# Windowed attention and a gated convolution feed-forward on one core: pairs of 64-token tiles and engine queues from a table

## The chip, the cores and the metric

One core of a Trainium2 chip runs the whole program in one launch. The metric is the device time of a run in microseconds; of several runs the median is taken. The engines have short names here: PE is TensorE (matrix products into PSUM), DVE is VectorE, ACT is ScalarE, POOL is GpSimd, SP is SyncE, whose queue issues nearly all DMAs.

## The reference

The inputs are q, k, v of shape (8, 8, 576, 64) (batch, head, token, feature) and three weights. All are fp32, and so is the output, (8, 576, 512).

```python
# attention within 32 tokens on either side
scores = q @ k.T / sqrt(64)
scores = where(abs(pos_q - pos_k) <= 32, scores, -1e9)
attn = exp(scores - max); attn = attn / (sum(attn) + 1e-9)
x = concat_heads(attn @ v)                      # (8, 576, 512)
# gated feed-forward with a convolution of three taps over the tokens
h = relu(x @ w_in)                              # w_in (512, 1024)
c = conv_w[0]*h[t-1] + conv_w[1]*h[t] + conv_w[2]*h[t+1]   # zero beyond a batch's ends
y = (h * sigmoid(c)) @ w_out                    # w_out (1024, 512)
```

## The kernel before

**Attention** goes by pairs of heads (`g`, 32 in all: 8 batches of 4 pairs). The 576 tokens are nine tiles of 64 queries, and each needs the 128 keys from 32 before its first token on. `load_qk` (L103) brings q or k of four heads in one DMA, with nine neighbouring tokens in one run; `load_v` (L95) brings v in blocks of 128 tokens, shifted by 32. `cast` (L109) turns each loaded tile into bf16 on POOL. Odd tiles need v shifted by 64 more tokens: `shift_v` copies `ve` to `vo` by two DMAs a batch (on DVE for batch 0). `job_tr` (L229, L236) transposes q or k of four heads by matmuls with an identity, nine for each pair of heads; ACT and DVE each copy one half out of PSUM. `job_sc` (L257 to L268) does 18 score matmuls for a pair of heads into one tile of three PSUM banks (`pa`) and one bank (`pf`), ACT takes the exponential (1088 and 64 columns), DVE multiplies by the mask. `job_av` (L282 to L301) does 20 matmuls; a column of ones in v gives the sum; DVE takes the reciprocal and scales into `xn`. `job_xt` (L312 to L324) transposes x to `xT`, by PE for batches 0 and 1 and by a DMA transpose for the others.

**Feed-forward** goes by chunks of 384 tokens (12) and blocks of 128 hidden features (`m`, 8 to a chunk). `job_ph` (L349 to L369) is four matmuls and a relu on ACT into `hT`. `job_pc` (L387 to L392) does the three taps of the convolution as three matmuls with diagonal weights, ACT takes tanh into an fp32 tile `tn` in SBUF, and DVE makes the gate product `(tn + 1) * hT`, with the halves of the sigmoid folded into the weights. `job_py` (L405 to L412) is eight matmuls for each 128 tokens, a copy on ACT and a store.

**Order.** Each job has a due time written by hand and a list of jobs that come before it; `give_out` hands the jobs out in the order of these times. In the first stage the order of instructions on PE, ACT and DVE is fixed (`InOrder`, whose calls all show as L87), later the scheduler of the framework may move them. POOL and SP keep the order in which the jobs are handed out. PSUM tiles come from two pools: one of three banks and five of one bank.

Of the kernel before, what the change touches and what calls it, by code (L numbers as in the profile page):

```python
# [9 lines left out]
FP32 = mybir.dt.float32  # L11
BF16 = mybir.dt.bfloat16
AF = mybir.ActivationFunctionType
ALU = mybir.AluOpType


@with_exitstack
def kernel(
# [21 lines left out]
    CH = 2 * S // 3  # L40
    HW = CH // 2
    PAD = 32
    RP = S // 64

    consts = ctx.enter_context(tc.tile_pool(name="consts", bufs=1))
    pp = ctx.enter_context(tc.tile_pool(name="pp", bufs=1))
    apool = ctx.enter_context(tc.tile_pool(name="apool", bufs=3))
    fpool = ctx.enter_context(tc.tile_pool(name="fpool", bufs=2))
    spool = ctx.enter_context(tc.tile_pool(name="spool", bufs=3))
    psum_a = ctx.enter_context(tc.tile_pool(name="psum_a", bufs=1, space=bass.MemoryType.PSUM))  # L50
    psum_f = ctx.enter_context(tc.tile_pool(name="psum_f", bufs=5, space=bass.MemoryType.PSUM))

    NLD = 2
    NPH = NP // 2
    qkst = [[pp.tile([128, 2, RP, 64], FP32, name=f"{n}st{i}") for i in range(NPH)] for n in "qk"]
    vst = pp.tile([128, NBLK, H, 64], FP32, name="vst")
    qkb_pp = [
        [[pp.tile([128, RP, 2, 64], BF16, name=f"{n}b{i}{j}") for j in range(NPH)] for n in "qk"]
        for i in range(NLD)
    ]  # L60
    ve_pp = [pp.tile([128, NBLK, H, 65], BF16, name=f"ve{i}") for i in range(NLD)]
    vo_pp = [pp.tile([128, NBLK - 1, H, 65], BF16, name=f"vo{i}") for i in range(NLD)]
    NKT = 4
    kT_pp = [pp.tile([128, S + 2 * PAD], BF16, name=f"kT{i}") for i in range(NKT)]
    hT_pp = [pp.tile([128, MB, CH + (4 if i == 1 else 2)], BF16, name=f"hT{i}") for i in range(3)]

    w_in_sb = consts.tile([128, KC, d_ff], BF16, name="w_in_sb")
    w_out_sb = consts.tile([128, MB, d_model], BF16, name="w_out_sb")
    conv_w_sb = consts.tile([128, 3, MB], FP32, name="conv_w_sb")
    diag_w = consts.tile([128, 3, MB, 128], BF16, name="diag_w")  # L70
    ident = consts.tile([128, 128], BF16, name="ident")
    mask = consts.tile([128, 2 * S], BF16, name="mask")
    mask1 = consts.tile([128, NT, 64], BF16, name="mask1")

    fixed = tc.keep_in_program_order

    class InOrder:


        on = False  # L80

# [3 lines left out]
        def __getattr__(self, name):  # L85
            do = getattr(self.engine, name)
            return (lambda *args, **kwargs: fixed(do(*args, **kwargs))) if InOrder.on else do  # L87

    vector, scalar, tensor = InOrder(nc.vector), InOrder(nc.scalar), InOrder(nc.tensor)

    def load_v(b, c):

        lo = 128 * c - PAD
        s0, s1 = max(0, lo), min(S, lo + 128)
        fixed(nc.sync.dma_start(  # L95
            vst[s0 - lo:s1 - lo, c, :, :], v[b, :, s0:s1, :].rearrange("h p d -> p h d")
        ))

    def load_qk(b, y, i):


        src = (q, k)[y][b, 4 * i:4 * i + 4, :, :]
        fixed(nc.sync.dma_start(  # L103
            qkst[y][i].rearrange("p e j d -> p e (j d)"),
            bass.AP(src.tensor, src.offset, [[RP * D, 128], [2 * S * D, 2], [1, RP * D]]),
        ))

    def cast(out_, in_):
        fixed(nc.gpsimd.tensor_scalar(  # L109
            out=out_, in0=in_, scalar1=1.0, scalar2=0.0, op0=ALU.mult, op1=ALU.add  # L110
        ))

    def load_stream(b):

        i = b % NLD
        ve, vo = ve_pp[i], vo_pp[i]

        def cast_v(c):
            cast(ve[:, c, :, 0:64], vst[:, c, :, :])
            if b == 0 and c > 0:  # L120
                vector.tensor_copy(vo[0:64, c - 1, :, :], ve[64:128, c - 1, :, :])
                vector.tensor_copy(vo[64:128, c - 1, :, :], ve[0:64, c, :, :])

        of_qk = [
            (lambda y=y, j=j: load_qk(b, y, j),
             lambda y=y, j=j: cast(qkb_pp[i][y][j].rearrange("p j e d -> p e j d"), qkst[y][j]))
            for j in range(NPH) for y in range(2)
        ]
        of_v = [(lambda c=c: load_v(b, c), lambda c=c: cast_v(c)) for c in range(NBLK)]
        return of_qk + of_v  # L130

    def shift_v(b):

        ve, vo = ve_pp[b % NLD], vo_pp[b % NLD]
        for p0, src in ((0, ve[64:128, 0:NBLK - 1]), (64, ve[0:64, 1:NBLK])):
            fixed(nc.sync.dma_start(vo[p0:p0 + 64], src))


    nc.vector.memset(vst[0:PAD, 0, :, :], 0.0)
    nc.vector.memset(vst[128 - PAD:128, NBLK - 1, :, :], 0.0)  # L140
    loads0 = list(load_stream(0))
    for ld, _ in loads0:
        ld()
    conv_w24 = consts.tile([3 * MB, 128], FP32, name="conv_w24")
    nc.scalar.dma_start(conv_w24, moe_conv_w.rearrange("k (m p) -> (k m) p", p=128))
    make_identity(nc, ident)
    ident24 = consts.tile([3 * MB, 3 * MB], FP32, name="ident24")
    nc.vector.tensor_copy(out=ident24, in_=ident[0:3 * MB, 0:3 * MB])
    nc.vector.memset(mask1, 1.0)
    nc.gpsimd.affine_select(  # L150
        out=mask1, in_=mask1, compare_op=ALU.is_ge, fill=0.0, base=0,
        pattern=[[0, NT], [-1, 64]], channel_multiplier=1,
    )
    nc.gpsimd.affine_select(
        out=mask1, in_=mask1, compare_op=ALU.is_ge, fill=0.0, base=64,
        pattern=[[0, NT], [1, 64]], channel_multiplier=-1,
    )
    nc.vector.memset(mask1[0:PAD, 0, :], 0.0)
    nc.vector.memset(mask1[128 - PAD:128, NT - 1, :], 0.0)
    for e in range(2):  # L160
        nc.vector.tensor_copy(
            out=mask[:, 512 * e:512 * e + 512], in_=mask1[:, 0:8, :].rearrange("p t x -> p (t x)")
        )
        nc.vector.tensor_copy(out=mask[:, 1024 + 64 * e:1088 + 64 * e], in_=mask1[:, 8, :])
    for t_ in ve_pp + vo_pp[0:1]:
        nc.vector.memset(t_[:, :, :, 64], 1.0)
    for t_ in kT_pp:
        nc.vector.memset(t_[:, 0:PAD], 0.0)
        nc.vector.memset(t_[:, PAD + S:], 0.0)
    nc.vector.memset(hT_pp[0][:, :, 0], 0.0)  # L170
    nc.vector.memset(hT_pp[1][:, :, HW + 1:HW + 3], 0.0)
    nc.vector.memset(hT_pp[2][:, :, CH + 1], 0.0)
    def make_diag(m):
        for kk in range(3):
            vector.tensor_scalar(
                out=diag_w[:, kk, m, :], in0=ident,
                scalar1=conv_w_sb[:, kk, m:m + 1], scalar2=None, op0=ALU.mult,
            )

    def load_weight(src, dst, rows, cast_):  # L180

        n = src.shape[1] // 2
        for x in (0, n):
            st = {}

            def load(x=x, st=st):
                t_ = fpool.tile([128, rows * n], FP32, name="wst", tag="wst")
                st[0] = t_.rearrange("p (c f) -> p c f", c=rows)
                fixed(nc.sync.dma_start(
                    st[0], src.rearrange("(c p) f -> p c f", p=128)[:, :, x:x + n]  # L190
                ))

            def casts(x=x, st=st):
                step = 512 // n
                for c in range(0, rows, step):
                    cast_(dst[:, c:c + step, x:x + n], st[0][:, c:c + step])

            yield load, casts


    def slot_a():
        return psum_a.tile([128, 1536], FP32, name="pa", tag="pa")

    def slot_f():
        return psum_f.tile([128, 512], FP32, name="pf", tag="pf")

    xT, xn = {}, {}
    state = {}

    def job_tr(g2, y):  # L210

        b, i = g2 // NPH, g2 % NPH
        nat = qkb_pp[b % NLD][y][i]
        to = []
        for g in (2 * g2, 2 * g2 + 1):
            if y == 0:
                t_ = apool.tile([128, S], BF16, name="qT", tag="qT", bufs=4)
                to.append(t_)
            else:
                t_ = kT_pp[g % NKT]  # L220
                to.append(t_[:, PAD:PAD + S])
            state["qk"[y], g] = t_

        small = b == 0
        for js in ((range(0, 4), range(4, 8), range(8, RP)) if small else (range(RP),)):
            j0, n = js[0], len(js)
            ps = slot_f() if small else slot_a()
            for j in js:
                tensor.matmul(  # L229
                    ps[:, 128 * (j - j0):128 * (j - j0) + 128],  # L230
# [352 lines left out]
```

## Time and profile before

| | |
|---|---|
| runs (us) | 270.17, 272.04, 279.48; median 272.04 |
| profiled execution: span | 271.7 |
| instructions | 6447 |
| granted clock of PE over the span | 0.978 |
| HBM read, written | 32.52 MB, 9.44 MB |
| issues on SP | q and k 32, v 40, `vo` shifts 14, DMA transposes 30, weights 4, stores 36 |

The profiled execution has a span of 271.7 us, 0.3 us below the median of the runs. A busy time counts each moment once, although neighbouring instructions of an engine overlap a little. Weight loads of PE (PEld) overlap its matmuls. Idle time of an engine that doesn't bound a stage costs nothing there.

### The profile page before, as it was taken

How to read it: one execution, taken by the hardware profiler on the slowest of the kernel's cores; microseconds unless marked ns; L12 is line 12 of the kernel's file. 1: busy time of each engine (PE TensorE's matmuls, PEld its weight loads, DVE VectorE, ACT ScalarE, POOL GpSimd, SP SyncE). 2: the span in 40 equal slices, each digit the busy share in tenths (PEclk: the TensorE clock that was granted, in tenths of full speed). 3: DMA queues.
4: the chain of work that ended last, by engine and by line, in shares of the span. 5: the costliest groups of instructions: out<-in, count | busy, mean ns of one | idle time of the engine just before them, and what ended most of it. 6: DMA issues, size and time to landing. Idle time of an engine off the chain costs nothing.

```text
span 271.7 us, 6447 instructions
## 1 busy us (share of the span) xinstructions
PE 236.4 (87%) x2535; PEld 143.5 (53%) x2562; DVE 160.5 (59%) x362; ACT 175.3 (65%) x370; POOL 81.0 (30%) x96
## 2 busy tenths in 40 slices
PE   1736974786999978998999999999999999999994
PEld 1625543574665544554555556565656455555551
DVE  5797385895466673765766656676666562323230
ACT  2755572585577663876777777777778567657552
POOL 5758656873026201233323432322300000000000
PEclk9999998998999997999999999999999999999998
DMA  7999999997377986399959988967546114312123
GB/s 258 256 344 358 198 296 321 224 309 164 100 183 253 222 151 165 110 287 242 208 146 319 159 196 257 294 112 177 152 121 89 40 41 109 98 39 77 41 77 116
DMA packets 70498, 49.64 MB, mean 183 GB/s; under 512 B 53676, under 2 KB 55748, under 8 KB 70468
## 3 DMA queue, kind: packets, MB, share of 16 engines
q1 hardware_dynamic: 70432, 49.22, 70.6%
q8 instruction: 20, 0.33, 0.6%
q14 instruction: 10, 0.08, 0.1%
q10 hardware_dynamic: 36, 0.01, 0.0%
HBM read 32.52 MB, written 9.44 MB: 154 GB/s over the span
## 4 chain that ended last, share of the span: by engine, by line
PE 68%; DMA 15%; DVE 5%; SPq 4%; ACT 3%; issue 2%; POOL 0%
PE pf L405 22%; PE pf L349 20%; PE pf L387 14%; DMA kst<-in_k_dram 5%; PE pa L229 4%; DMA vst<-in_v_dram 4%; PE pf L282 4%; DMA vo<-ve 3%; PE pa L257 3%; DMA xT<-xn 3%; SPq L95 2%; DVE attn L268 1%; SPq L312 1%; DVE gT L392 1%; DVE diag_w L87 1%
## 5 line engine op out<-in xcount | busy, mean ns | idle before, releaser
L392 DVE SCALAR_TENSOR_TENSOR gT<-tn,hT 128x384 bf16<-128x384 f32 (+1 forms) x96 | 55.7, 585 | 55.7 <-ACT tn L391 55.6
L349 PE MATMUL pf<-xT,w_in_sb 128*128 128x385 bf16 (+2 forms) x380 | 73.6, 317 | 4.9 <-DMA xT<-xn 3.7
L405 PE MATMUL pf<-w_out_sb,gT 128*128 128x512 bf16 x261 | 66.5, 385 | 1.7 <-issue 0.4
L387 PE MATMUL pf<-hT,diag_w 128*128 128x384 bf16 (+1 forms) x288 | 59.0, 314 | 0.7 <-ACT hT L360 0.6
L349 PEld LDWEIGHTS <-w_in_sb 128*128 128x128 bf16 x380 | 34.4, 98 | 25.9 <-issue 3.3
L410 ACT COPY y_sb<-pf 128x512 f32<-128x512 f32 x36 | 21.1, 586 | 40.8 <-PE pf L405 40.8
L391 ACT ACTIVATE tn<-pf 128x384 f32<-128x384 f32 (+1 forms) x96 | 44.9, 469 | 2.3 <-PE pf L387 1.9
L109 POOL TENSOR_SCALAR ve<-vst 128x512 bf16<-128x512 f32 x40 | 28.9, 724 | 55.2 <-DMA vst<-in_v_dram 42.9
L405 PEld LDWEIGHTS <-gT 128*128 128x128 bf16 x288 | 28.0, 99 | 30.4 <-issue 1.6
L387 PEld LDWEIGHTS <-diag_w 128*128 128x128 bf16 x288 | 26.1, 98 | 17.1 <-issue 1.2
L369 ACT ACTIVATE hT<-pf 128x385 bf16<-128x385 f32 x56 | 27.7, 496 | 10.8 <-PE pf L349 10.1
L266 ACT ACTIVATE attn<-pa 128x1088 bf16<-128x1088 f32 x26 | 27.9, 1074 | 4.7 <-PE pf L257 3.9
L109 POOL TENSOR_SCALAR qb<-qst 128x1152 bf16<-128x1152 f32 x16 | 19.9, 1242 | 26.8 <-DMA qst<-in_q_dram 26.8
L268 DVE TENSOR_TENSOR attn<-attn,mask 128x1152 bf16<-128x1152 bf16 x26 | 20.9, 804 | 10.4 <-ACT attn L267 9.6
L109 POOL TENSOR_SCALAR kb<-kst 128x1152 bf16<-128x1152 f32 x16 | 18.9, 1182 | 21.9 <-DMA kst<-in_k_dram 21.1
L301 DVE TENSOR_TENSOR xn<-pf,rec 128x320 bf16<-128x320 f32 x52 | 24.3, 486 | 0.8
L364 ACT ACTIVATE hT<-pf 128x386 bf16<-128x386 f32 x24 | 11.9, 494 | 4.4 <-PE pf L349 4.0
L282 PEld LDWEIGHTS <-attn 128*64 128x64 bf16 x520 | 10.7, 112 | 7.3 <-issue 5.6
L282 PE MATMUL pf<-ve,attn 128*64 128x65 bf16 x312 | 13.8, 199 | 0.3 <-DVE attn L268 0.3
L257 PEld LDWEIGHTS <-kT 64*128 64x128 bf16 x468 | 9.0, 95 | 7.9 <-issue 5.5
L257 PE MATMUL pa<-qT,kT 64*128 64x64 bf16 x442 | 12.3, 191 | 0.9 <-DVE kT L236 0.9
L282 PE MATMUL pf<-vo,attn 128*64 128x65 bf16 x208 | 12.9, 200 | 0.0
(84 smaller groups left out, 240.1 us busy)
## 6 DMA issues: line engine op xcount, KB each, us to landing
qst<-in_q_dram SPq DMA_DIRECT2D x16, 576.0 KB, 6.4
kst<-in_k_dram SPq DMA_DIRECT2D x16, 576.0 KB, 7.4
out_dram<-y_sb SPq DMA_DIRECT2D x36, 256.0 KB, 2.2
vst<-in_v_dram SPq DMA_DIRECT2D x24, 256.0 KB, 4.7
vo<-ve SPq DMA_DIRECT2D x14, 260.0 KB, 7.8
vst<-in_v_dram SPq DMA_DIRECT2D x16, 192.0 KB, 5.0
wst<-in_moe_w_in_dram SPq DMA_DIRECT2D x2, 1024.0 KB, 8.4
wst<-in_moe_w_out_dram SPq DMA_DIRECT2D x2, 1024.0 KB, 8.9
```

Source lines behind the costliest of these rows:

```text
L109: fixed(nc.gpsimd.tensor_scalar(out=out_, in0=in_, scalar1=1.0, scalar2=0.0, op0=ALU.mult, op1=ALU.add))
L257: tensor.matmul(last[:, 0:64] if e * t == NT - 1 else ps[:, col(e, t):col(e, t) + 64], kT[64 * e:64 * e + 64, 64 * t:64 * t + 128], qT[64 ...
L266: scalar.activation(attn[:, 0:x], ps[:, 0:x], AF.Exp, bias=0.0, scale=scale)
L268: vector.tensor_tensor(out=attn, in0=attn, in1=mask, op=ALU.mult)
L282: tensor.matmul(pss[e][64 * j:64 * j + 64, 65 * c:65 * c + 65], attn[:, col(e, t):col(e, t) + 64], (ve if t % 2 == 0 else vo)[:, t // 2, h ...
L301: vector.tensor_tensor(out=to, in0=po[:, :, 0:64], in1=rec[:, :, None].broadcast_to([128, NBLK, 64]), op=ALU.mult,)
L349: tensor.matmul(ps[:, 0:n], w_in_sb[:, kc, m * 128:(m + 1) * 128], x_[:, kc, x0:x1], start=(kc == 0), stop=(kc == KC - 1),)
L369: scalar.activation(hT[:, m, o0:o0 + n], ps[:, 0:n], AF.Relu, bias=0.0, scale=0.5)
L387: tensor.matmul(ps[:, 0:n], diag_w[:, kk, m, :], taps(kk), start=(kk == 0), stop=(kk == 2))
L391: scalar.activation(tn[:, 0:n], ps[:, 0:n], AF.Tanh, bias=0.0, scale=1.0)
L392: vector.scalar_tensor_tensor(out=gT[c][:, m, HW * halves[0]:HW * halves[0] + n].rearrange("p (i x) -> p i x", x=HW), in0=tn[:, 0:n].rearr ...
L405: tensor.matmul(ps, gT[c][:, m, 128 * i:128 * i + 128], w_out_sb[:, m, :], start=(m == 0), stop=(m == MB - 1),)
```

## The change

The function is written anew; names of DRAM tensors, weights in bf16 and the tanh form of the gate stay. What differs:

- **The order** is a table. `PROGRAM` is a string of some 1480 words; each names a step, the engine where there is a choice (A ACT, V DVE, P POOL, D for a PE step that leaves a tap to DVE), its indices, and behind @ its PSUM banks. All instructions of all five engines are kept in program order. All PSUM is one tile of eight banks.
- **Attention by pairs of tiles.** The 72 query tiles of the 8 batches make 36 pairs, and each step takes one pair for all eight heads: `sc` (16 matmuls into two banks), `ex` (one exponential of 1024 columns, in 23 pairs into bf16 in SBUF and in 13 in place in PSUM), `mk` (mask, from either), `av` (16 matmuls), `rc`, `nm`. The x transpose is on PE for 24 pairs (`xp`, `xc`) and by DMA for 12 (`xt`).
- **q and k** are loaded with tokens 2p and 2p+1 on partition p, in runs of 512 bytes, 256 tokens of all heads to a tile (64 in the third); 24 DMAs each. The transposes use the transpose form of a matmul into bf16 PSUM, eight to a tile (two for the third), and one copy (`eq`, `ek`) takes a tile out, on ACT or DVE.
- **vo** is copied by DVE in all batches (34 instructions) and no more by DMA.
- **Chunks** have 1, 2, 3 (ten times), 2 and 1 pairs of 128 tokens; there are 14, so 112 blocks of chunk and hidden features.
- **The convolution** of a block has one of three forms: three taps on PE (17 blocks); two taps on PE and the middle one added by DVE in PSUM (55); no tap on PE (40), each tap scaled on ACT (46) or POOL (74) into fp32 tiles in SBUF and two sums on POOL (80).
- **tanh** is written to PSUM in fp32, in place or from the sum, and the gate product reads it there.
- Casts of loads are mostly on POOL (82 of q, k and v), a few on ACT and DVE; y is copied out by ACT (19) and DVE (17).

The diff, cut to its core (the old functions are above):

```diff
+CHUNKS = """1 2 3 3 3 3 3 3 3 3 3 3 2 1"""
+PROGRAM = """
+s_hpad s_ident lk.0.1 lcw s_vpad lk.0.2 s_mask lk.0.0 s_mask2 lv.0.0 lq.0.0 s_kpad lv.0.2 lv.0.1 s_ones lwi.2
...
+m1.0.2@2 th.1.0@7 dt.0.3@3 kv.1.4P@4 cq.1.1P th.1.5@5 gt.1.0@7 m1.1.1@6 rl.0.2@2 th.0.3@3 lv.1.3 gt.1.5@5
...
+"""
+    def load(src, n, b, i):
+        t = st[n, i]
+        if i < 2:
+            s = src[b, :, 256 * i:256 * i + 256, :]
+            dims = [[2 * D, 128], [S * D, H], [1, 2 * D]]
...
+        sync.dma_start(t.rearrange("p h j d -> p h (j d)"), bass.AP(s.tensor, s.offset, dims))
...
+    def ov(e, bk, b, c, n):
+        vector.tensor_copy(out=vo[b % 2][0:64, c:c + n], in_=ve[b % 2][64:128, c:c + n])
+        vector.tensor_copy(out=vo[b % 2][64:128, c:c + n], in_=ve[b % 2][0:64, c + 1:c + 1 + n])
...
+    def turn(n, bk, i):
+        ...
+                tensor.transpose(o[:, c:c + 128],
+                                 t[:, j, 2 * pr:2 * pr + 2, :].rearrange("p h d -> p (h d)"), ident)
...
+    def sc(e, bk, i):
+        for pr in range(NP):
+            for tp in range(2):
+                b, t = divmod(2 * i + tp, NT)
+                for f in range(2):
+                    w = kT[b % 2][64 * f:64 * f + 64, pr, 64 * t:64 * t + 128]
+                    c = 128 * pr + 64 * tp
+                    tensor.matmul(ps[:, bk[f], c:c + 64], w,
+                                  qT[b % 2][64 * f:64 * f + 64, pr, 64 * t:64 * t + 64],
+                                  start=True, stop=True)
...
+    def ex(e, bk, i):
+        scores = two(bk[0], bk[1], [[1, 512]])
+        to = attn[i % NA].rearrange("p (f r) c -> p f (r c)", f=2) if e == "A" else scores
+        scalar.activation(to, scores, AF.Exp, bias=0.0, scale=scale)
...
+    def kv(e, bk, c, m):
+        o0, o1, n = span(c)
+        taps = {"P": (0, 1, 2), "D": (0, 2)}[e]
+        for kk in taps:
+            tensor.matmul(ps[:, bk[0], 0:n], diag_w[:, kk, m, :], hT[:, m, o0 + kk - 1:o1 + kk - 1],
+                          start=(kk == taps[0]), stop=(kk == taps[-1]))
...
+    def dt(e, bk, c, m):
+        o0, o1, n = span(c)
+        vector.scalar_tensor_tensor(out=ps[:, bk[0], 0:n], in0=hT[:, m, o0:o1], scalar=tap(1, m),
+                                    in1=ps[:, bk[0], 0:n], op0=ALU.mult, op1=ALU.add)
+
+    def ta(e, bk, c, m, kk, s):
+        o0, o1, n = span(c)
+        o, i = tt[s][kk][:, 0:n], hT[:, m, o0 + kk - 1:o1 + kk - 1]
+        if e == "A":
+            scalar.activation(o, i, AF.Copy, bias=0.0, scale=tap(kk, m))
+        else:
+            gpsimd.tensor_scalar(out=o, in0=i, scalar1=tap(kk, m), scalar2=0.0, op0=ALU.mult, op1=ALU.add)
+
+    def tb(e, bk, c, m, kk, s):
+        n = span(c)[2]
+        gpsimd.tensor_tensor(out=tt[s][0][:, 0:n], in0=tt[s][0][:, 0:n], in1=tt[s][kk][:, 0:n], op=ALU.add)
+
+    def th(e, bk, c, m, s=None):
+        n = span(c)[2]
+        src = ps[:, bk[0], 0:n] if s is None else tt[s][0][:, 0:n]
+        scalar.activation(ps[:, bk[0], 0:n], src, AF.Tanh, bias=0.0, scale=1.0)
+
+    def gt(e, bk, c, m):
+        o0, o1, n = span(c)
+        for x0, x1 in ((o0, S + 1), (S + 2, o1)) if o0 <= S < o1 - 1 else ((o0, o1),):
+            g0 = x0 - 1 - (x0 > S)
+            vector.scalar_tensor_tensor(
+                out=gT[:, m, g0:g0 + x1 - x0], in0=ps[:, bk[0], x0 - o0:x1 - o0], scalar=1.0,
+                in1=hT[:, m, x0:x1], op0=ALU.add, op1=ALU.mult)
...
+    steps = dict(locals())
+    for word in PROGRAM.split():
+        word, _, banks = word.partition("@")
+        e = word[-1] if word[-1] in "AVPD" else ""
+        name, *args = (word[:-1] if e else word).split(".")
+        steps[name](e, [int(x) for x in banks], *[int(x) for x in args])
```

There is one buffer for each loaded tile of q, k and v (`st`, `vst`), two of each `ve`, `vo`, `qT`, `kT`, five of `attn`, three of `xn` and of y, and one of `xT`, `hT` and `gT`, which hold two batches.

## The prediction

> **What bounds the kernel now.** I read four views in this order. First the page's line of busy times and the table of stages (columns: stage, length, then busy time and instruction count of PE, PEld, DVE, ACT, POOL, then the granted clock, DMA share, GB/s):
>
> ```profile
> PE 236.4 (87%) x2535; PEld 143.5 (53%) x2562; DVE 160.5 (59%) x362; ACT 175.3 (65%) x370; POOL 81.0 (30%) x96
> ```
>
> ```profile
> 0.00:25.00 25.00, 10.79 (x192) 9.03 (x192) 19.71 (x68) 12.51 (x32) 16.36 (x26) 1.00 1.02 305
> 25.00:45.00 20.00, 13.47 (x138) 8.51 (x137) 11.34 (x29) 10.45 (x25) 13.10 (x17) 1.00 0.99 259
> ...
> 65.00:85.00 20.00, 19.08 (x237) 12.52 (x238) 10.80 (x26) 12.57 (x34) 4.86 (x7) 0.91 0.63 169
> 85.00:105.00 20.00, 16.93 (x179) 9.62 (x181) 11.50 (x23) 12.08 (x24) 5.78 (x6) 0.95 0.77 173
> ...
> 185.00:205.00 20.00, 19.77 (x233) 11.61 (x234) 12.96 (x28) 14.97 (x31) 4.23 (x5) 1.00 0.63 150
> ```
>
> PE is the bound in every stage after 45 us: 19.77 us of 20 at 185 to 205, while DVE has 65%, ACT 75% and POOL 21%. Before 45 us PE has only half its time, while DVE is full (19.71 of 25) and the loads come in. So two things can shorten this kernel: less PE work, and an earlier full start.
>
> Second, the chain that ended last gives the price of each PE job when PE streams (start, length, what, count):
>
> ```profile
> 137.51 0.49 PE pf L387 x3
> 138.00 0.66 PE pf L349 x4
> 139.15 0.36 PE pa L257 x17
> 139.52 0.44 PE pf L282 x20
> 141.21 0.50 PE pa L229 x9
> 215.60 1.73 PE pf L405 x8
> ```
>
> So a conv block (three taps) is 0.49 us, 0.163 a tap; a `w_in` block 0.66; a `w_out` row block 1.73; a 128-column transpose 0.0556; a score matmul 0.021; an AV matmul 0.022. Third, the timeline gives what one instruction of the other engines costs, and how two collide:
>
> ```profile
> 160.08 0.49 ACT L391 ACTIVATE tn<-pf 128x384 f32<-128x384 f32 x1
> 160.47 1.07 ACT L266 ACTIVATE attn<-pa 128x1088 bf16<-128x1088 f32 x1
> 195.61 0.76 DVE L236 CAST qT<-pa 128x576 bf16<-128x576 f32 x1 [0.76 <-ACT qT L236]
> 196.28 0.55 DVE L392 SCALAR_TENSOR_TENSOR gT<-tn,hT 128x384 bf16<-128x384 f32 x1
> 202.10 0.76 DVE L268 TENSOR_TENSOR attn<-attn,mask 128x1152 bf16<-128x1152 bf16 x1 [1.18 <-ACT attn L267]
> 136.22 1.13 DVE L268 TENSOR_TENSOR attn<-attn,mask 128x1152 bf16<-128x1152 bf16 x1 [0.46 <-ACT attn L267]
> 34.27 0.62 POOL L109 TENSOR_SCALAR ve<-vst 128x512 bf16<-128x512 f32 x1 [0.45 <-DMA vst<-in_v_dram]
> 136.12 1.70 POOL L109 TENSOR_SCALAR ve<-vst 128x512 bf16<-128x512 f32 x2 [1.22 <-DMA vst<-in_v_dram]
> ```
>
> The reader sees two things. Packed instructions overlap: ACT's next starts 0.39 after a start of 0.49, DVE's next 0.67 after a start of 0.76, so about 0.10 (ACT) and 0.08 (DVE) of each is free. And DVE and POOL lock each other out: the mask product takes 0.76 alone but 1.13 when the `ve` casts run, and those two take 1.70 instead of 1.24. Products that read PSUM are not touched (`xn` 0.49 with POOL busy and idle).
>
> **The change part by part.** From these rows: ACT 0.168 us + 0.85 ns an element (0.222 at 64, 0.494 at 385); DVE at one element a cycle 0.153 + 1.04 ns (0.49 at 320, 0.76 at 576); POOL 0.193 + 0.833 ns (0.62 at 512, 1.15 at 1152). I counted the words of the table with the sizes of their tiles.
>
> *PE.* `w_in`: 96 blocks of 0.655 become 112 smaller ones with the same columns, 62.9 to 62.6. `w_out` is the same, 36 x 1.73 = 62.2. Transposes of q and k stay 288, 16.0. Scores stay 576, 11.8. AV falls from 640 to 576, 14.1 to 12.7. The x transposes rise from 40 to 96, 2.2 to 5.3. Conv: 17 blocks keep three taps, 55 keep two, 40 have none, so 161 taps of 288: 47.0 to 22.2. Sum: 216.2 to 192.8, 23.4 us less.
>
> *ACT.* relu 112 (50.2), tanh 112 (50.2), exp 36 x 1.04 (37.4), q and k out of PSUM 26 (22.4), taps 46, `xT` and y copies 30 (18.1), rest 9.5. A tap multiplies by a pointer; the row `xn<-pf,rec` (0.358 at 64 against 0.222 for exp) puts 0.136 on it: 26.8. Sum 214.6 in durations, 176.3 with 0.10 off each of 383.
>
> *DVE.* gate products 144 (60.4; the four chunks that cross a batch need two each), middle tap `dt` 55 (27.6), masks 36 (31.6: 23 of bf16 at two a cycle, 13 out of PSUM), `rc` and `nm` (31.3), q and k copies 22 (19.6), `xT` and y 30 (20.6), `vo` copies 34 (14.0, at the rate of the mask copy, 512 in 0.288), rest 5.4: 210.5, or 177.9 with 0.08 off each of 409. It takes over the `vo` shift, 14 DMAs of 260 KB. Of this, 35.2 us in 72 instructions (bf16 masks, `vo`, casts, diagonals) has all its big operands in SBUF and falls under the lock. The gate product no longer does: tanh now stays in PSUM.
>
> *POOL.* casts 62.1; taps 74 (35.0); sums `tb` 80 of 329 elements on average. No row has a two-input POOL instruction: at least one pass of a cast (0.468 each, 37.4 in all), at most two whole casts one after the other (0.936, 74.9). I take two passes and one fixed part, 0.748, 59.9: both inputs are fp32 like the casts' one. POOL then has 157, and 192 with the locked DVE work.
>
> The Trainium skill, "GPSIMD Engine Reference", section "Elementwise — side-by-side cycle accounting", speaks against the sums: it gives 4497 ns for a two-input add of 2048 fp32, so an estimate of 0.92 us at 329 elements with POOL's fixed part; by it POOL would have 13 us more than in my sum. No run here shows it yet.
>
> *Transposes* of q, k and x now use the transpose form; no row shows that form. By the nearest row (identity matmul) it costs 0.0556; if it were as slow as the slowest such group, at the start (nine from 11.96 us, the next nine 0.94 later), it would be 0.104, and 384 would add 19. I take the row of the steady part, where all but the first few run. "TensorE: Matmul & The Clock Gate", section "Part 4: PE-mode transpose", says that such transposes do not count as activity for the clock; by that alone the granted clock would fall around the blocks of 8, which the third rival prices from rows.
>
> *Loads.* q and k come in runs of 512 bytes instead of 2304. At the start, the five v loads (runs of 256) hold SP from 3.0 to 11.3 us: 1.18 MB in 8.3, 142 GB/s; the page's first slice, with q and k, has 258. The 2.36 MB that the first pairs need take 9 to 17 us; I take 10, as 512 is above v's 256. After the last q lands: cast 1.05, transposes 0.45, copy 1.22, scores 0.33, exp 1.04, mask 1.22, AV 0.35, `rc` 0.18, `nm` 0.69, transpose 0.22, copy 0.69, some 7.5 us and a hand-over of 0.15 between each. The first `w_in` block then starts at 20 us (bounds 18 to 27; before: 28.6).
>
> *Sum.* PE has 4.8 us behind it at 20 us and 188.0 ahead. DVE has 165.4 ahead, and lock waits: a POOL instruction is in progress about 68% of the time and half of its 0.7 is left, 0.24 for each of 60, so 180. ACT has 166, POOL with the locked work 182. PE is still the longest, but by 5%, not by 35%, so hand-overs cost more: PE had 0.99 where the others had 65 to 75%, and 0.90 at 65 to 105 us (36.0 of 40). I choose 0.88, just under the worse row, since all queues are now fixed by hand: 188.0 / 0.88 = 213.6. The last y copy and its store take 3 (0.59 + 2.2). 20 + 213.6 + 3 = 237. At 0.95 it is 221, at 0.82 252. The sum is made against the profiled span of 271.7, which is 0.3 below the median of the runs, 272.04; I add nothing for that.
>
> **Rivals.** *DVE becomes the bound.* If its instructions don't overlap and each locked one waits out most of a POOL instruction (0.47), it has 195.7 + 28 = 224 ahead; at 0.95 that is 236, so 259. For it: the lock row, and POOL goes from 30% to some 68%. Against it: the overlap stands in each packed stretch of the timeline.
>
> *The clock falls.* At 65 to 85 us the granted clock was 0.91 with PE at 95%; if sparse PE work brings that throughout, 188 / 0.91 / 0.88 = 235, so 258. Against: 25 to 45 us had 1.00 with PE at 67%.
>
> *In-order queues* (the slow side). POOL now casts loads and computes taps in one fixed order, and SP's fixed order puts loads behind y stores. A late load holds up every tap behind its cast, the tanh that waits for them, and the PSUM bank. Today's waits for loads:
>
> ```profile
> POOL ve L109 <- DMA vst<-in_v_dram: 42.9, 23, 7.5
> POOL qb L109 <- DMA qst<-in_q_dram: 26.8, 14, 6.1
> POOL kb L109 <- DMA kst<-in_k_dram: 21.1, 12, 4.9
> ```
>
> That is 90.8 us, free today as POOL is idle anyway. If all came back on a POOL with 182 ahead: 20 + 182 + 91 + 3 = 296. It is slower than before by 2% (277.5) from 72 of the 91. Against it: 3.6 MB of `vo` copies leave the DMA queues, and a wait exists only while the loads are late.
>
> **How the numbers follow.** My forecast (222 to 252) has 0.57, DVE 0.15, clock 0.08, queues 0.20, of which 0.08 ends within 2% of before and 0.12 above. So faster 0.80, same 0.08, slower 0.12; 2% is about what a measurement here can tell. The range goes from 220 (0.95, with a start at 19) to 268, past DVE and clock into the mildest queue case.
>
> **What would show it.** Right: conv matmuls of 161 in place of 288; ACT near 180 busy, DVE 180 to 200, POOL 150 to 175; the first `xT` matmul near 20 us; PE at 85 to 90% after it. `tb` near 0.75 (0.47 or 0.94 would put POOL elsewhere), gate products near 0.55 whatever POOL does, bf16 masks over 0.72 when it is busy. Wrong: PE under 80% with POOL or DVE waiting for DMA, or transposes of 0.104.

## The result and the profile after

The changed kernel takes 299.81 us (median; 296.9 to 301.78), the kernel before 273.72 (median of four): ratio 1.102, 95% interval 1.085 to 1.120. The ratio leaves out disturbed runs on both sides, so it is not the quotient of the medians. Forecast were 237 us, at most 268. It is slower by 10%. The profiled execution has a span of 297.9 us, and its run took 299.62.

The page of the changed kernel, busy times and granted clock in 40 slices:

```profile
PE 228.3 (77%) x2435; PEld 144.9 (49%) x2435; DVE 198.5 (67%) x427; ACT 190.2 (64%) x384; POOL 172.2 (58%) x248
PEclk9999888598999999897999899658559999999999
```

Every engine has about the work that was forecast, and none is full. PE was to lose 23.4 us of work and lost 8 of busy time (236.4 to 228.3), since the clock is lower: 0.908 over the span, 0.978 before. (In the split kernel below, at 0.979, the same matmuls are busy for 212.1, which is 24.3 less.) One stage of the changed kernel (columns as before):

```profile
185.00:205.00 20.00, 12.92 (x173) 9.18 (x172) 10.31 (x19) 11.02 (x15) 8.32 (x12) 0.66 0.33 87
```

At 185 to 205, where PE before had 19.77 us of 20, PE is idle a third of the time and the other three about half of it, and the clock is at 0.66. When nothing is full, something passes from engine to engine one at a time. The timeline of the changed kernel inside that stage shows it:

```profile
190.21 1.02 ACT L182 ACTIVATE attn<-ps 128x1024 bf16<-128x1024 f32 x1 [0.76 <-PE ps L182]
...
191.27 1.23 DVE L182 TENSOR_TENSOR attn<-ps,mask 128x1024 bf16<-128x1024 f32 x1 [0.85 <-ACT attn L182]
192.54 1.01 PE L182 MATMUL ps<-ident,xn 128*128 128x128 bf16 x8 [2.01 <-DVE attn L182]
...
193.59 1.02 ACT L182 ACTIVATE attn<-ps 128x1024 bf16<-128x1024 f32 x1 [2.36 <-PE ps L182]
194.65 0.76 DVE L182 COPY xT<-ps 128x512 bf16<-128x512 bf16 x2 [2.16 <-ACT attn L182]
194.67 1.04 PE L182 MATMUL ps<-qT,kT 64*128 64x64 bf16 x32 [1.11 <-ACT attn L182]
```

Read the releasers against the code. The transposes at 192.54 take `xn`, yet they wait 2.01 us for a mask product, which writes `attn`. The copy of `xT` at 194.65 waits for an exponential. These belong to different pairs and share no data. In the table the steps are `ex.23A@45`, `mk.27@71`, `xp.21@2`, `ex.24A@06`, `xc.22V@3` and `sc.25@45`, and the semaphore waits of the built program say:

```
mask product, banks 1 and 7    waits for   exponential, banks 4 and 5
transposes into bank 2         wait for    mask product, banks 1 and 7
exponential, banks 0 and 6     waits for   mask product, banks 1 and 7, and transposes into bank 3
xT copy out of bank 3          waits for   exponential, banks 0 and 6
scores into bank 4             wait for    exponential, banks 0 and 6
```

No two share a bank. In each line one instruction spans two banks, and the other's bank lies between them. All PSUM is one tile, and `ex`, `mk` (out of PSUM), `rc` and `nm` read two banks in one instruction:

```python
def two(x, y, dims, off=0):
    return apx(ps[:, x, off:off + 1], [[512 * (y - x), 2]] + dims)
```

So the framework orders such an instruction against everything from the lower bank to the upper. I compared every semaphore wait of the built program with the elements that instructions really read and write: 145 waits between engines protect no data, not even through a chain of other waits. In 134 of them one side is such a span and the other side's bank lies between its ends; five more are weight loads that carry the wait of their matmul; six have other causes. Of the 36 score pairs only 12 have neighbouring banks, and 10 lie six apart; of the 36 AV pairs 15 are neighbours. The waits after, some that carry data among them (engine, tile, line, releaser; sum, times, longest):

```profile
...
PE ps L182 <- DVE xn L182: 15.0, 14, 2.2
PE ps L182 <- ACT attn L182: 14.4, 12, 1.9
...
ACT attn L182 <- DVE xn L182: 7.6, 6, 2.1
...
POOL ve L182 <- DMA vst<-in_v_dram: 7.1, 3, 5.4
```

The first two hold waits of both sorts, as a transpose does need its own `xn`. The `attn <- xn` line is unneeded throughout: an exponential reads scores and writes `attn`, and the scaling into `xn` touches neither. In the split kernel below, `ps <- xn` is 3.0 us, and the other two are no longer among its longest sixty. The last line is the load wait which the in-order rival feared, 42.9 us before; with those of POOL for q (9.6) and k (1.1), 17.8 us are left of 90.8.

### The profile page after: what moved, and what is told of

It is laid out like the page before. It is cut to its first block, busy times and chain, and to the rows that moved or that the text cites. A ratio compares the mean times of both kernels' runs of the same rounds, so it can differ in the third digit from the quotient of the medians.

```text
span 297.9 us, 6469 instructions
## 1 busy us (share of the span) xinstructions
PE 228.3 (77%) x2435; PEld 144.9 (49%) x2435; DVE 198.5 (67%) x427; ACT 190.2 (64%) x384; POOL 172.2 (58%) x248
## 5 line engine op out<-in xcount | busy, mean ns | idle before, releaser
L182 PE MATMUL ps<-xT,w_in_sb 128*128 128x384 bf16 (+2 forms) x448 | 79.5, 326 | 8.2 <-ACT attn L182 2.9
L182 POOL TENSOR_SCALAR t<-hT,conv_w_sb 128x385 f32<-128x385 bf16 (+4 forms) x74 | 41.6, 571 | 63.5 <-ACT hT L182 58.6
L182 POOL TENSOR_TENSOR t<-t,t 128x385 f32<-128x385 f32 (+4 forms) x80 | 72.0, 906 | 10.3 <-ACT t L182 8.5
L182 PE MATMUL ps<-w_out_sb,gT 128*128 128x512 bf16 x288 | 69.6, 393 | 4.7 <-DVE xn L182 3.0
L182 DVE SCALAR_TENSOR_TENSOR gT<-ps,hT 128x193 bf16<-128x193 f32 (+6 forms) x144 | 54.6, 419 | 17.8 <-ACT ps L182 12.0
L182 ACT ACTIVATE hT<-ps 128x384 bf16<-128x384 f32 (+2 forms) x112 | 47.2, 450 | 14.2 <-PE ps L182 8.7
L182 ACT ACTIVATE ps<-ps 128x385 f32<-128x385 f32 (+5 forms) x85 | 43.1, 521 | 14.8 <-PE ps L182 6.8
L182 DVE SCALAR_TENSOR_TENSOR ps<-hT,conv_w_sb,ps 128x385 f32<-128x385 bf16 (+4 forms) x55 | 29.9, 565 | 22.7 <-PE ps L182 13.3
L182 ACT ACTIVATE attn<-ps 128x1024 bf16<-128x1024 f32 x23 | 23.6, 1024 | 25.8 <-PE ps L182 9.9
L182 PE MATMUL ps<-hT,diag_w 128*128 128x385 bf16 (+4 forms) x161 | 31.3, 307 | 3.2 <-ACT attn L182 1.9
L182 DVE TENSOR_TENSOR xn<-ps,rec 128x512 bf16<-128x512 f32 x36 | 24.2, 682 | 10.6 <-ACT attn L182 5.2
L182 ACT ACTIVATE t<-hT,conv_w_sb 128x385 f32<-128x385 bf16 (+3 forms) x46 | 25.5, 566 | 0.5
L182 PEld LDWEIGHTS <-kT 64*128 64x128 bf16 x576 | 13.1, 104 | 18.7 <-issue 13.3
```

Source lines behind the costliest of these rows:

```text
L182: return lambda *args, **kwargs: fixed(do(*args, **kwargs))
```

## The experiments

Theory A: the waits without data cost the time, and the lower clock follows from them. Rivals: the written order costs it (B), the detour of the taps over ACT and POOL (C), or the slower clock as a cause of its own. Later texts name their own rivals.

**The same instructions, other banks.** Only digits behind @ differ (859 of 1482 words), so that every pair is of neighbours; 8 unneeded waits are left of 145.

```diff
-sc.1@56 sc.0@70 ... ex.1P@56 ... mk.1@56 ... ex.0P@70
+sc.1@67 sc.0@12 ... ex.1P@67 ... mk.1@67 ... ex.0P@12
```

> Only the bank digits of the table are changed: the two banks of each score tile and of each AV tile are now neighbours. All instructions, their engines and their order stay. In the changed kernel an access to banks 6 and 0 makes the program wait as if it touched banks 0 to 6; 145 of the waits between engines have no shared data behind them, with neighbours 8. Theory A (these unneeded waits hold the engines up): 240 to 262 us, with PE at half clock for under 25 us of the span instead of 56. Theory B (hand-overs of a hand-fixed order, with the data it really needs): 292 to 303. Theory C (taps on POOL come late) and theory D (the half clock itself): 292 to 303 too, since neither POOL's work nor the sparseness of PE's work is touched.

Measured: 253.8 us, ratio to before 0.931 [0.924, 0.939], clock 0.972. If the clock is always full or half, that is some 14 us at half clock (2 x 0.028 x 251.6), an estimate, where Theory A said under 25. The time is 46 us less than the changed kernel, with the same instructions, order and shapes. Groups of the changed kernel (busy, mean ns, then idle time before and releasers):

```profile
L182 DVE TENSOR_TENSOR xn<-ps,rec 128x512 bf16<-128x512 f32 x36 | 24.2, 682 | 10.6 <-ACT attn L182 5.2 <-PE ps L182 1.9 <-ACT ps L182 1.9
L182 ACT ACTIVATE attn<-ps 128x1024 bf16<-128x1024 f32 x23 | 23.6, 1024 | 25.8 <-PE ps L182 9.9 <-DVE xn L182 7.6 <-DVE rec L182 4.3
...
L182 DVE SCALAR_TENSOR_TENSOR gT<-ps,hT 128x385 bf16<-128x385 f32 x24 | 12.7, 551 | 2.0 <-ACT ps L182 1.8
```

and of the one with neighbouring banks:

```profile
L182 DVE TENSOR_TENSOR xn<-ps,rec 128x512 bf16<-128x512 f32 x36 | 23.9, 684 | 0.4
L182 ACT ACTIVATE attn<-ps 128x1024 bf16<-128x1024 f32 x23 | 23.1, 1025 | 10.2 <-PE ps L182 9.6 <-DVE xn L182 0.5
```

A read over far banks costs the engine nothing: 1024 and 1025 ns, 682 and 684. Only the idle time ahead differs, 25.8 to 10.2 and 10.6 to 0.4. Theory A stands; B, C and a clock that falls by itself do not, as order, taps and transposes are the same in both.

**One bank for each instruction.** The banks of the table stay, but each two-bank instruction becomes two; 6 unneeded waits are left. DVE has 85 instructions more, ACT 36.

```diff
-        scores = two(bk[0], bk[1], [[1, 512]])
-        to = attn[i % NA].rearrange("p (f r) c -> p f (r c)", f=2) if e == "A" else scores
-        scalar.activation(to, scores, AF.Exp, bias=0.0, scale=scale)
+        for f in range(2):
+            scores = ps[:, bk[f], :]
+            to = attn[i % NA].rearrange("p (f r) c -> p f (r c)", f=2)[:, f] if e == "A" else scores
+            scalar.activation(to, scores, AF.Exp, bias=0.0, scale=scale)
```

(and `mk`, `rc`, `nm` in the same way)

> The bank numbers stay, but each instruction that touched two banks is split into two of one bank: exp, masks out of PSUM, reciprocals and scalings by the sums. That removes the same unneeded waits (6 left of 145) in another way, and adds 36 fixed parts on ACT (about 6 us) and 85 on DVE (about 13 us). Theory A: 248 to 272, a little above the kernel with neighbouring banks. Theories B, C, D: 300 to 312, the old time and what the split adds.

Measured: 247.94 us, ratio 0.908 [0.900, 0.916], clock 0.979. It does more work than the changed kernel and takes 52 us less, just under the lower end expected. The banks are those of the changed kernel, so it is not another choice of banks that gains. Its busy times, and the stage at 185 to 205 us:

```profile
PE 212.1 (86%) x2435; PEld 134.2 (55%) x2435; DVE 205.2 (83%) x512; ACT 187.9 (76%) x420; POOL 176.6 (72%) x248
185.00:205.00 20.00, 18.51 (x161) 9.95 (x154) 17.79 (x44) 13.70 (x31) 17.45 (x22) 1.00 0.37 74
```

**Half of the cure.** First `ex` and `mk` alone split, then `rc` and `nm` alone.

```diff
 split ex, mk: as above        split rc, nm: as in the changed kernel     (83 unneeded waits)
 split ex, mk: as in the changed kernel        split rc, nm: as above     (85 unneeded waits)
```

> Only the exponentials and the mask products out of PSUM are split by bank; reciprocal and normalization still span two far banks: 83 of the 145 unneeded waits stay. Theory A with every wait of like weight: 300 - 52 x 62/139 = 277, so 268 to 286. Rival D (only those of the long ACT instructions matter): 248 to 258. Rival E (only those of VectorE's reciprocal matter): 290 to 302.

Measured: 267.33 us.

> The other half: reciprocal and normalization are split by bank, exponentials and mask products still span two far banks: 85 of the 145 unneeded waits stay. Theory A with every wait of like weight: 300 - 52 x 60/139 = 278, so 268 to 286. Rival D (only those of the long ACT instructions matter): 290 to 302. Rival E (only those of the reciprocal matter): 248 to 258.

Measured: 281.09 us. The gains are 299.8 - 267.3 = 32.5 and 299.8 - 281.1 = 18.7, together 51.2 against 51.9 for both at once. They add up, within the scatter of a few us that the runs have (266.2 to 268.5 and 280.8 to 281.4 here, 296.9 to 301.8 for the changed kernel): each half has its own waits. Theory A's range just missed the first and holds the second. But the waits of the exponentials and masks weigh more than the count says (62 waits of the 145 for 32.5 us, 60 for 18.7), so equal weight does not hold; D and E are refuted.

**The rest of the change, with and without these waits.** Two parts were undone twice, in the changed kernel and in the split one. The 40 blocks without a tap on PE get their three taps on PE back:

```diff
-ta.0.7.0.0P ... ta.0.7.2.0P ... tb.0.7.2.0 ... ta.0.7.1.0P ... tb.0.7.1.0 ... th.0.7.0@4
+kv.0.7P@4 th.0.7@4
```

> The 40 blocks whose taps were scaled on ACT and POOL and summed on POOL get three taps on PE, put right in front of their tanh; POOL keeps only casts. PE gains 40 x 0.43 = 17 us, ACT loses 27, POOL 110. Theory C (taps on POOL late): 265 to 285. Theory A: 285 to 305, the unneeded waits stay and PE has more to do. Theory B: 285 to 305.

Measured in the changed kernel: 316.52 us, 16.7 more than with the taps shared out, and more than A or B said: extra PE work isn't hidden although PE is idle nearly a quarter of the time. By the two profiles PE's busy time rises by 17.1 (228.3 to 245.4) and its idle time stays (69.6 and 69.2). A's range, about the changed kernel's own time, left no room for that; why the idle time doesn't take the work up was not followed up.

> The kernel with two-bank instructions split (247.9 us) and, on top, all 40 blocks that POOL and ACT compute given back to TensorE with three taps each: TensorE has about 17 us more work, POOL and ACT lose their taps. Theory A (without the waits that carry no data TensorE sets the time at 0.85 of it): 17 / 0.85 = 20 us more, 258 to 270. Rival C (the taps' detour through ACT, POOL and PSUM is what still holds the kernel up): 240 to 250.

Measured in the split kernel: 261.28 us, 13.3 more than 247.9, with PE at 231.8 busy. The share-out is worth 13 to 17 us in both, so C is refuted in both. And the order of PE, DVE and ACT is left to the scheduler:

```diff
-    vector, scalar, tensor = InOrder(nc.vector), InOrder(nc.scalar), InOrder(nc.tensor)
+    vector, scalar, tensor = nc.vector, nc.scalar, nc.tensor
```

> PE, ACT and DVE are no longer held to the order of the table; the framework's scheduler may move their instructions (POOL and SP stay). Some 270 lines of each engine's order change. Theory B (the fixed order): 270 to 288. Theory A: 290 to 305, as the unneeded waits come with any order. Theory C: 290 to 305.

Measured in the changed kernel: 327.43 us, 27.6 slower. B is refuted with the wrong sign, and A's number was too low as well.

> The split kernel (247.9 us) with the order of TensorE, VectorE and ScalarE left to the scheduler; POOL and SP keep theirs. In the changed kernel this cost 27 us (300 to 327). Theory A: that 27 came from the waits across banks, which a free order meets more of; without them it costs little, 245 to 256. Rival B2: the order written out is worth its 27 us by itself, 268 to 282.

Measured in the split kernel: 265.39 us, 17.5 slower, between the two expectations. So the written order is worth 17 us by itself; what the other 10 were, the waits or the scheduler's other choices, is not separated.

**The best version.** Adjacent banks cost 6 us more than split instructions. Three versions ran on one chip:

> Both cures together: pairs of neighbouring banks in the table and two-bank instructions split by bank. Adjacent banks alone gave 253.8 us, splitting alone 247.9. Theory F (splitting is the better one because the next engine can begin after half of the work and each bank comes free earlier): 246 to 250. Rival G (the other choice of banks costs the 6 us, a reused bank comes free later): 252 to 257.

> Table as in the changed kernel; the two-bank instructions are split only where the two banks are not neighbours, so some 40 per cent of them keep one instruction and its single fixed cost. Theory F (half-way hand-over is worth more than the fixed cost of a second instruction): 248 to 253. Rival H (the second fixed cost, 0.2 us on ACT and 0.14 on VectorE, is what counts): 241 to 247.

```diff
+        if abs(bk[1] - bk[0]) == 1:   # neighbours: one instruction, as in the changed kernel
+            ...
+            return
         for f in range(2):
```

> The split kernel once more, on the chip of the two others: 246 to 250 by its first run (247.9). All theories expect the same; it is there so that a difference of 2 per cent between the three versions can be read.

Measured: 254.59, 248.71 and 247.92 us; ratios to before 0.930 [0.925, 0.936], 0.910 [0.905, 0.915] and 0.908 [0.903, 0.913]. With neighbouring banks splitting gains nothing (253.8 to 254.6), so the 6 us are the price of that choice of banks and not of the longer instruction: Theory F is refuted, and G's range holds the time. Keeping one instruction where banks are neighbours changes nothing that can be told, so the second fixed cost, rival H, isn't what counts either. The split kernel beats the kernel before by 9% and the changed one by 17% (247.9 / 299.8 = 0.827).

## Why the prediction was wrong, by its steps

**Work sums: right within 6%.** ACT near 180 was 190.2, DVE 180 to 200 was 198.5, POOL 150 to 175 was 172.2; 161 conv matmuls. Gate products that read PSUM take 0.551 as forecast (0.55). Transposes cost 0.0575 each at full clock (in the split kernel sixteen take 1.07 us and eight 0.61, so eight more take 0.46), against the 0.0556 taken.

**`tb`: mis-sized.** 0.748 was taken at 329 elements (two passes and a fixed part come to 0.74 by the prediction's own rates); the 80 measured 0.906 on average, inside the bounds and near the upper one. That is 72.0 us of POOL where the sum had 59.9. "GPSIMD Engine Reference", section "Elementwise — side-by-side cycle accounting" of the Trainium skill, gave an estimate of 0.92 and was right against my choice; the measured 0.906 is what to carry.

**The start: wrong, and by the same cause.** The first `w_in` block was to start at 20 us. First the changed kernel, then the split one (matmuls of the tile in the first 32 us: shortest, median, longest, first and last start):

```profile
L182 PE MATMUL ps<-xT,w_in_sb x24: 266/311/311, 28.6 to 31.3; 128*128 128x128 bf16 x24
```

```profile
L182 PE MATMUL ps<-xT,w_in_sb x46: 218/292/311, 22.3 to 31.9; 128*128 128x128 bf16 x32, 128*128 128x256 bf16 x14
```

Without the unneeded waits it is 22.3, with the same loads. My chain for it (exp, mask, AV, `rc`, `nm`, transpose) added the steps of one pair; in the changed kernel several pairs run at once and wait for each other. Two readings behind the start were loose. DVE was called full before 45 us, at 19.71 of 25 us and then 11.34 of 20. And PE was called the bound in every stage after 45 us, but from 45 to 65 us DVE is busier, 17.32 us against PE's 15.65.

**The efficiency of 0.88: the step that failed.** It stood for hand-overs, taken from stages of the kernel before, where each step had PSUM tiles of its own. In the changed kernel waits without data came on top, which no term of the sum held. 28.6 + 3 us aside, 266.3 us remain for the 188.0 of PE work: 0.706. In the split kernel 246.2 - 22.3 - 3 = 220.9, so 0.851. Of the 61.3 us that the profiled span lies above the unrounded sum of 236.6, the start's 8.6 and the stretch's 52.7, splitting takes back 51.7 (6.3 and 45.4). 2.3 at the start and 7.3 in the stretch remain; the heavier `tb` and the added instructions are in there, not separated.

The 0.88 also mixed two measures. The rows behind it, 0.99 and 0.90, are busy shares, but it divides a sum of prices, and for the kernel before that sum is 216.2 where the page has PE busy for 236.4. Counted as those rows count, PE of the split kernel is busy for 202.5 of the 220.9 us, a share of 0.92. So without the unneeded waits the hand-overs cost no more than forecast, and the 7.3 us that remain are less than the 14.5 by which busy time exceeds the 188.0.

**The rivals.** The in-order queues were given 296 us, close to the measured time, but for another reason: they were to wait for loads, and POOL's waits for loads fell to 17.8 us. DVE isn't the bound. The clock's 0.91 came true (0.908), but as a follower: with the same transposes and other banks it is 0.972. Of the 51.7 us by which splitting shortens the span, PE's busy time accounts for 16.2 (228.3 to 212.1, the same matmuls) and its idle time for 35.5; how much of that idle time the slower matmuls themselves brought is not separated. "TensorE: Matmul & The Clock Gate", section "Why this matters for your kernels" of the Trainium skill, warns of PE gaps over about 3 us. Here the granted clock of the changed kernel, 1.00 from 185 to 189 us, fell to 0.50. In the 3 us before, PE had one gap of 0.80 us, up to 187.12, and was in the one of 1.99 (below, two stages and then PE's row behind it), so sparse work with shorter gaps is enough:

```profile
185.00:190.00 5.00, 2.21 (x71) 1.53 (x71) 2.48 (x7) 3.42 (x6) 5.00 (x7) 0.91 0.42 159
190.00:195.00 5.00, 1.88 (x43) 1.65 (x39) 1.99 (x4) 2.05 (x2) 3.32 (x6) 0.50 0.78 167
```

```profile
189.50 0.72 PE L182 MATMUL ps<-qT,kT 64*128 64x64 bf16 x20 [1.99 <-ACT ps L182]
```

None of the rivals was a wait made by the framework, though the view that shows it, the waits of the built program, needs no chip. The diff held the sign: one tile for all PSUM, and `two()` with banks as far apart as 0 and 7.

## What to carry to other kernels

An access with a large stride across a tile that other instructions use can be ordered against everything between its ends. When a change gathers buffers into one tile, list the waits of the built program and ask of each which element both sides touch, before summing any work. In a profile the sign is a releaser that shares no tile with the waiter while every engine is half idle; the cure is one instruction per buffer (248 us here) or neighbouring buffers (254), not less work.

## What the runs showed of the hardware

The lock between DVE and POOL is common where POOL is busy, and can be long. I had 0.24 us for each of 60 locked instructions, 14 us in all, and masks "over 0.72". The median of the bf16 mask hides it: 0.683 in the changed kernel and 0.693 in the split one. But the mean in the split kernel is 0.950:

```profile
L182 DVE TENSOR_TENSOR attn<-attn,mask 128x1024 bf16<-128x1024 bf16 x23 | 21.6, 950 | 1.2 <-ACT attn L182 0.9
...
L182 DVE COPY vo<-ve 64x1056 bf16<-64x1056 bf16 (+1 forms) x34 | 19.0, 559 | 1.3 <-POOL ve L182 0.5
```

Ten of these 23 masks took 0.73 us or more, each with POOL at work beside it, and 14 of the 34 copies took over 0.5 where the others took 0.43 or less. Masks at 0.68, 30 copies at 0.43 and four at 0.29 would be 29.7 us; the 40.6 measured are 11 more, an estimate of what the lock cost. In the changed kernel, where POOL is idle more, only three masks took over 0.72. One mask of the split kernel took 3.85 us; its timeline:

```profile
158.15 3.85 DVE L182 TENSOR_TENSOR attn<-attn,mask 128x1024 bf16<-128x1024 bf16 x1
...
158.72 2.38 POOL L182 TENSOR_SCALAR ve<-vst 128x512 bf16<-128x512 f32 x4
```

POOL worked without a gap from 155.63 to 161.46, and the mask ended at 162.00, 0.54 us after that. "SBUF — State Buffer", section "SBUF: two separate sides" of the Trainium skill, says that the loser of the shared port blocks for the other's whole instruction; this run shows it waiting through a row of them.
